# Windowed attention and a gated feed-forward on one core: two chunks of attention in one stretch of small matmuls

## The chip, the cores and the metric

The kernel runs on one core of a Trainium2 chip. A core has a matrix engine (TensorE, "PE" in the profile; its weight loads are listed apart as "PEld"), three engines for elementwise work (VectorE "DVE", ScalarE "ACT", GpSimd "POOL") and a queue engine ("SP") that here only issues DMAs. Each works through its own instructions in order, and they wait for one another on semaphores. Matmul results go to PSUM, eight banks of 128 x 512 fp32, from which DVE and ACT read them. The metric is the device time of one execution in microseconds. Three runs of the kernel before gave 337.34, 338.25 and 338.31 us; the median is 338.25.

## The reference

```python
# q, k, v: (8, 8, 576, 64) fp32;  window = 64
scores = (q @ k^T) / sqrt(64)
mask = (0 <= i - j) & (i - j < 64)
attn = softmax(where(mask, scores, -1e9))
x = (attn @ v).transpose(0, 2, 1, 3).reshape(4608, 512)
g = x @ w_gate                      # 512 -> 1536
out = (silu(g) * (x @ w_val)) @ w_out   # 1536 -> 512, fp32
```

Each token attends to itself and the 63 before it in its own sequence. All 4608 tokens then go through the feed-forward part.

## The kernel before

The tokens are cut into 36 chunks of 128 (index n) for attention and nine groups of 512 (index c) for the feed-forward part. Sequences are 576 long, so some chunks hold a boundary, and a part of their window is left out. Matmuls run in bf16.

**Attention of a chunk.** `load_qk` and `load_v` have POOL load q, k and v (cast to bf16) into rings of buffers; `TD(n)` (line 414) lets two DMA transposes on SP's queue turn k and q into `kT` and `qT`. `S(n)` (line 435) computes the scores: 24 matmuls of 64x64 (line 451) into two banks, an exp on ACT for each bank (line 461) that writes the weights `pt`, and a multiplication by the mask on DVE for each (line 466), which can be deferred. `A(n, nxt)` (line 472) multiplies weights and values: 32 matmuls of 64x64 (line 500) into two banks, four heads in each. A window of 64 queries meets two blocks of 64 keys, which lie in different halves of the partitions, and the two halves may not write one bank at the same moment. So the work is in two phases of 16: in phase 0 the first bank gets the lower half and the second the upper, in phase 1 the other way round, and phase 1 waits for a semaphore that phase 0 raises. A 65th column of the values is 1 and yields the sums for the softmax: DVE takes the reciprocal (line 515) and multiplies (line 518) into `xb`. The scores of the next chunk are issued between the two phases. `XD(n)` (line 543) transposes `xb` by DMA on SP's queue into `xT`.

**Feed-forward.** `F(c, f)` (line 550) computes 128 of the 1536 hidden columns for a group: four matmuls of 128x128 by 512 with `Wg` into bank G, four with `Wv` into bank V (line 565), a tanh on ACT (line 571) and two operations on DVE (lines 573 and 575) that leave `hT`; the first of these releases G, the second V. `O(c, u)` (line 578) multiplies a quarter of the group's `hT` by `Wo` in twelve matmuls (line 589); ACT copies the result to `ost` (line 601) and SP's queue writes it out.

**Order.** The order of every engine is the order of the calls in `build` (line 753). A call records operations with what they read and write, and the program derives the semaphore waits. In the main loop group c has four steps u of three F calls each (s = 0, 1, 2); between them come one `O` of the group before (after the second F) and, from the table `place`, one attention block (`block`, line 868): loads for chunk n + 6, `A(n, n + 1)`, `XD(n)`, `TD(n + 4)`. From chunk 17 on the block follows the first F of each step. In the last group `O` of the step u = 3 comes later, and `judge` (line 626) decides between this program and a general one that covers inputs with large scores; with the reference's inputs the general one is not taken.

**Banks.** `bank(kind)` (line 262) hands out PSUM banks in turn from two rings of four: "f" for F, "a" for attention and O. Whoever writes a bank again waits for its last reader.

## Time and profile before

| | |
|---|---|
| median of three runs | 338.25 us (337.34 to 338.31) |
| the profiled execution | 338.46 us |
| its span, first to last instruction | 336.6 us |
| mean granted TensorE clock | 0.995 |
| data read from and written to HBM | 37.75 MB and 9.44 MB |

The profile is one execution recorded by the hardware. Rows of the page give busy time, share of the span and the number of instructions. A row of the timeline gives start and duration in microseconds, engine, line of the code, operation, output and inputs, shapes and the number of merged instructions; in brackets stands the idle time of that engine just before and what ended it. "64*64" is the part of the array that a matmul uses, and what follows is the moving operand. A row of the waits names who waited for whom, the total, the number of times and the longest, all in microseconds. A row of the DMA issues ends with the median time from issue to landing.

### The profile page before, as it was taken

What the parts mean: (1) busy time and instruction counts of PE and PEld (TensorE: products, weight loads), DVE (VectorE), ACT (ScalarE), POOL (GpSimd) and SP (SyncE); (2) the same over time, 40 slices, a digit from 0 to 9 for tenths busy, and PEclk for the clock granted to TensorE, in tenths of its full rate; (3) what the DMA queues carried; (4) which work ended last, traced back from release to release, by engine and by line L of the source; (5) the groups of instructions that cost most, each with busy time, mean ns of one, the idle gap of its engine ahead of it and who ended that gap; (6) DMA issues with size and microseconds to landing.
All of it is one profiled execution on the core that took longest, in us unless ns stands there. A gap on an engine that the chain in (4) does not pass through costs nothing.

```text
span 336.6 us, 8417 instructions
## 1 busy us (share of the span) xinstructions
PE 325.6 (97%) x3515; PEld 166.1 (49%) x3515; DVE 215.6 (64%) x481; ACT 140.1 (42%) x256; POOL 111.1 (33%) x141
## 2 busy tenths in 40 slices
PE   6979999998999999999999999999999999999995
PEld 3548567644444444444444444444444444444444
DVE  5548789478667766666666666666666665566510
ACT  2645874354444544443433344433443332332311
POOL 7999993463544353333343333000000000000000
PEclk9979999999999999999999999999999999999999
DMA  9999999999999999999999999334331111000012
GB/s 170 143 186 171 167 195 160 154 177 128 172 179 180 177 154 166 162 168 127 125 80 149 139 139 126 80 79 80 78 80 49 47 49 49 31 32 34 34 65 95
DMA packets 169516, 40.20 MB, mean 119 GB/s; under 512 B 155904, under 2 KB 164992, under 8 KB 169472
## 3 DMA queue, kind: packets, MB, share of 16 engines
q0 software_dynamic: 117312, 18.36, 77.6%
q1 hardware_dynamic: 50976, 20.66, 34.0%
q10 hardware_dynamic: 1184, 0.59, 0.7%
q8 instruction: 29, 0.48, 0.5%
q14 instruction: 15, 0.12, 0.2%
HBM read 37.75 MB, written 9.44 MB: 140 GB/s over the span
## 4 chain that ended last, share of the span: by engine, by line
PE 87%; DMA 4%; POOL 4%; DVE 2%; ACT 1%; issue 1%; SPq 0%; POOLq 0%
PE ps L565 53%; PE ps L589 26%; PE ps L500 4%; DMA qT<-qn 2%; PE ps L451 2%; DMA Wv<-in_moe_w_val_dram 2%; POOL va L382 1%; PE ps L617 1%; POOL Wg L388 1%; PE ps L407 1%; POOL Wv L388 1%; POOL qn L320 1%; POOL kn L320 1%; DVE uu L573 0%; PE ps L532 0%
## 5 line engine op out<-in xcount | busy, mean ns | idle before, releaser
L573 DVE SCALAR_TENSOR_TENSOR uu<-sig,ps 128x512 bf16<-128x512 bf16 (+2 forms) x122 | 76.1, 624 | 82.6 <-ACT sig L571 82.4
L565 PE MATMUL ps<-xT,Wg 128*128 128x512 bf16 (+2 forms) x488 | 114.1, 356 | 2.0 <-DMA Wg<-in_moe_w_gate_dram 0.9
L565 PE MATMUL ps<-xT,Wv 128*128 128x512 bf16 (+2 forms) x488 | 113.8, 356 | 0.7 <-DMA Wv<-in_moe_w_val_dram 0.7
L589 PE MATMUL ps<-Wo,hT 128*128 128x512 bf16 x420 | 95.9, 379 | 0.0
L571 ACT ACTIVATE sig<-ps 128x512 bf16<-128x512 f32 (+2 forms) x122 | 66.9, 549 | 61.6 <-PE ps L565 61.1
L575 DVE SCALAR_TENSOR_TENSOR hT<-uu,ps 128x512 bf16<-128x512 bf16 (+2 forms) x122 | 76.3, 625 | 5.2 <-PE ps L565 1.0
L565 PEld LDWEIGHTS ps<-xT,Wv 128*128 128x128 bf16 x488 | 47.3, 98 | 47.7 <-DMA Wv<-in_moe_w_val_dram 1.0
L589 PEld LDWEIGHTS ps<-Wo,hT 128*128 128x128 bf16 x420 | 41.0, 98 | 48.9
L565 PEld LDWEIGHTS ps<-xT,Wg 128*128 128x128 bf16 x488 | 43.9, 98 | 42.3 <-DMA Wg<-in_moe_w_gate_dram 1.0
L320 POOL DMA_DIRECT2D qn<-in_q_dram x38 | 35.1, 941 | 85.9 <-DMA qT<-qn 85.6
L601 ACT ACTIVATE ost<-ps 128x512 f32<-128x512 f32 x35 | 20.9, 597 | 95.1 <-PE ps L589 92.2
L461 ACT ACTIVATE pt<-ps 128x512 bf16<-128x512 f32 x72 | 38.9, 595 | 22.6 <-PE ps L451 22.6
L382 POOL DMA_DIRECT2D va<-in_v_dram x40 | 37.2, 940 | 1.0 <-issue 0.6
L320 POOL DMA_DIRECT2D kn<-in_k_dram x38 | 35.0, 927 | 5.0 <-DMA Wo<-in_moe_w_out_dram 4.0
L518 DVE TENSOR_TENSOR xb<-ps,rc 128x256 bf16<-128x256 f32 x72 | 30.6, 425 | 2.5
L466 DVE TENSOR_TENSOR pt<-pt,mask 128x512 bf16<-128x512 bf16 x64 | 24.1, 417 | 0.2 <-ACT pt L461 0.2
L500 PE MATMUL ps<-va,pt 64*64 64x65 bf16 x1088 | 23.3, 199 | 0.6
L500 PEld LDWEIGHTS ps<-va,pt 64*64 64x64 bf16 x1088 | 15.3, 109 | 16.1 <-issue 11.2
L515 DVE RECIPROCAL rc<-ps 128x4 f32<-128x4 f32 x72 | 12.6, 175 | 9.9 <-PE ps L500 9.9
L451 PE MATMUL ps<-qT,kT 64*64 64x64 bf16 (+1 forms) x864 | 15.9, 201 | 1.0 <-DMA qT<-qn 1.0
L451 PEld LDWEIGHTS ps<-qT,kT 64*64 64x64 bf16 x864 | 12.6, 108 | 3.1 <-DMA qT<-qn 1.2
L339 DVE COPY ost<-ps 128x128 f32<-128x128 f32 x1 | 0.3, 291 | 11.8 <-PE ps L617 11.8
(50 smaller groups left out, 72.5 us busy)
## 6 DMA issues: line engine op xcount, KB each, us to landing
out_dram<-ost SPq DMA_DIRECT2D x35, 256.0 KB, 3.1
va<-in_v_dram POOLq DMA_DIRECT2D x32, 128.0 KB, 9.9
qn<-in_q_dram POOLq DMA_DIRECT2D x30, 128.0 KB, 11.2
kn<-in_k_dram POOLq DMA_DIRECT2D x30, 128.0 KB, 10.0
Wo<-in_moe_w_out_dram POOLq DMA_DIRECT2D x2, 768.0 KB, 17.4
Wg<-in_moe_w_gate_dram POOLq DMA_DIRECT2D x5, 256.0 KB, 8.0
Wv<-in_moe_w_val_dram POOLq DMA_DIRECT2D x5, 256.0 KB, 9.1
fk<-in_k_dram SPq DMA_DIRECT2D x1, 512.0 KB, 5.4
```

Of the source, the lines that this page charges most:

```text
L320: self.g.op("pool", lambda e, d=d, a=a: e.dma_start(d, a), writes=ks, dma=True)
L382: g.op("pool", lambda e, d=d, a=a: e.dma_start(d, a), writes=ks, dma=True)
L451: r = e.matmul(sv[h][o:o + 64, c, q0:q1], self.kT[ps, c, kk:kk + 64], qT[ps, c, q0:q1], start=not biased, stop=not biased or c == 3 and kk ...
L461: g.op("act", lambda e, po=po, si=si: e.activation(po, si, ACTF.Exp, scale=SCALE), reads=[bk], writes=[pk])
L466: "dve", lambda e: e.tensor_tensor(po, po, m, ALU.mult), reads=[pk, "mask"], writes=[pk]))
L500: r = e.matmul(av[half][ws, j, :], pt[ks, h, ws], vv[ks, h, 0:65], start=key == q[0], stop=key == q[-1])
L518: g.op("dve", lambda e, xo=xo, rb=rb, a=av[half]: e.tensor_tensor(xo, a[:, :, 0:64], rb, ALU.mult), reads=[bk, ("rc", ir)], writes=[("xb", ...
L565: r = e.matmul(bank[:, 0:n], W[:, kk, f * 128:f * 128 + 128], xT[:, kk, t0:t1], start=(kk == 0), stop=(kk == NK - 1))
L571: g.op("act", lambda e: e.activation(sig[:, 0:n], G[:, 0:n], ACTF.Tanh, scale=0.5), reads=[gk], writes=[("sig", i)])
L573: g.op("dve", lambda e: e.scalar_tensor_tensor(uu[:, 0:n], sig[:, 0:n], 1.0, G[:, 0:n], ALU.add, ALU.mult), reads=[("sig", i), gk], writes ...
L575: g.op("dve", lambda e: e.scalar_tensor_tensor(hT[:, f, t0:t1], uu[:, 0:n], 0.5, V[:, 0:n], ALU.mult, ALU.mult), reads=[("uu", i), vk], wr ...
L589: r = e.matmul(OB[:, :], hT[:, f, 128 * u:128 * u + 128], self.Wo[:, f, :], start=(f == 0), stop=(f == NF - 1))
```

## The change

Chunks below 20 are treated as before. From chunk 20 on:

- `pair(n)` takes the place of two blocks. It follows the third F and the `O` of every second step u, from (c, u) = (3, 3) for chunks 20 and 21 to (7, 1) for chunks 34 and 35. It issues the loads of chunks n + 6 and n + 7, the values of both chunks with the scores of n + 2 and n + 3 (`A_pair`), then `TD(n + 4)`, `TD(n + 5)`, `XD(n)`, `XD(n + 1)`, and the four masks at the end.
- `A_pair` uses three banks: heads 0 to 6 of the first chunk, heads 0 to 6 of the second, and the eighth heads of both. Scores of n + 2 come first, then phase 0 of both chunks, scores of n + 3, phase 1. In a phase the first chunk uses one half of the partitions and the second the other; the eighth heads both use the same half. Reciprocals and multiplications follow per bank, over seven heads at once, and for the eighth heads apart.
- From (3, 2) on, `O` moves behind the third F. In the steps with a pair DVE does its copy, in the others ACT.
- Right after the F call of (3, 2, 1) `S(20)` is issued alone, and `share` merges the two rings of banks into one of eight, from which everything is handed out from then on. After each pair but the last the order of the ring is set anew.

The score calls, read in order: block 19 still contains `S(20)`, the call at (3, 2, 1) is `S(20)` again, and the first pair issues `S(22)` and `S(23)`. No call issues `S(21)`; the values of chunk 21 are taken with the weights that stand in its buffer, those of chunk 17. The numbers of scores, exps and masks are what they were.

```diff
     def bank(self, kind):
+        kind = "*" if "*" in self.rot else kind
         ids, i = self.rot[kind]
...
+    def share(self):
+        j = [self.rot[k][0][self.rot[k][1] % 4:] + self.rot[k][0][:self.rot[k][1] % 4] for k in "fa"]
+        self.rot["*"] = ([x for p in zip(*j) for x in p], 0)
...
+    def A_pair(self, n, S0, S1):
+        g = self.g
+        nn = (n, n + 1)
+        masks = S0()
+        banks = [self.bank("a") for _ in range(3)]
+        pt = [self.pt[m % self.NP] for m in nn]
+        seqs, last = [[], []], {}
+        for step in range(2):
+            for h, i in [(h, i) for h in range(7) for i in range(2)] + [(7, 0), (7, 1)]:
+                kp = step if h == 7 else step ^ i
+                b, col = (2, 65 * i) if h == 7 else (i, 65 * h)
+                for w in range(2):
+                    if kp == w or (2 * nn[i] + w) % BPB:
+                        seqs[step].append((i, h, kp, w, b, col))
+                        last.setdefault((b, w), []).append((step, i, h))
...
+        first = g.op("pe", phase(0), reads=rd, writes=wr)
+        masks = masks + S1()
+        g.op("pe", phase(1), reads=rd, writes=wr, after=[first])
...
+            g.op("dve", lambda e, rc=rc, a=a: e.reciprocal(rc.unsqueeze(2), a[:, :, 64:65]), reads=[bk],
+                 writes=[("rc", 2 * m), ("rc", 2 * m + 1)])
...
+            g.op("dve", lambda e, xo=xo, rb=rb, a=a: e.tensor_tensor(xo, a[:, :, 0:64], rb, ALU.mult),
+                 reads=[bk, ("rc", 2 * m)], writes=[("xb", m % 4, 0), ("xb", m % 4, 1)])
...
+        return masks
...
-    def O(self, c, u, mid=None, kind="a"):
+    def O(self, c, u, mid=None, kind="a", eng="act"):
...
-        g.op("act", lambda e: e.activation(ost[:, :], OB[:, :], ACTF.Copy), reads=[ok], writes=[("ost", io)])
+        self.move(eng, ost[:, :], OB[:, :], [ok], [("ost", io)])
...
+        pair_from = 20
+
+        def pair(n):
+            ring, i = self.rot["*"]
+            ring = [ring[(i + j) % 8] for j in range(8)]
+            more = n + 2 < NCH
+            for m in (n + 6, n + 7):
+                load(m)
+            masks = self.A_pair(n, *(lambda m=m: self.S(m, None, True) if more else [] for m in (n + 2, n + 3)))
+            if more:
+                self.rot["*"] = ([ring[j] for j in (7, 0, 1, 5, 6, 2, 3, 4)], 0)
+            for m in (n + 4, n + 5):
+                if m < NCH:
+                    self.TD(m)
+            for m in (n, n + 1):
+                self.XD(m)
+            for f in masks:
+                f()
...
-        for n in range(17, NCH):
+        for n in range(17, pair_from):
             place[(n - 5) // 4, (n - 5) % 4, 0] = n
+        pairs = {}
+        for n in range(pair_from, NCH, 2):
+            c, r = divmod(n - 6, 4)
+            pairs[c, 1 + r] = n
+        alone = (pair_from - 6) // 4, (pair_from - 6) % 4, 1
+        cp = alone[0]
...
+                    if (c, u, s) == alone:
+                        self.S(pair_from)
+                        self.share()
-                    if s == 1 and not late:
+                    if s == 1 and not late and c < cp:
                         self.O(c - 1, u, None, "f" if (c, u, s) in place or (c, u) == (1, 1) else "a")
...
+                if c >= cp and not late:
+                    self.O(c - 1, u, None, "a", "dve" if (c, u) in pairs else "act")
+                if (c, u) in pairs:
+                    pair(pairs[c, u])
```

31 lines of the change are left out of this document (added).

## The prediction

> **What bounds the kernel now.** I read the page first, for the engine shares and the chain of waits.
>
> ```profile
> PE 325.6 (97%) x3515; PEld 166.1 (49%) x3515; DVE 215.6 (64%) x481; ACT 140.1 (42%) x256; POOL 111.1 (33%) x141
> PE 87%; DMA 4%; POOL 4%; DVE 2%; ACT 1%; issue 1%; SPq 0%; POOLq 0%
> ```
>
> TensorE (PE) is busy for 97% of the span and carries 87% of the chain that ended last. A busy PE need not be a PE at its peak, so next comes PE's timeline over one period of the part that is changed: three F calls, one O call and one attention block (chunk 29).
>
> ```profile
> 224.91 1.03 PE L565 MATMUL ps<-xT,Wv 128*128 128x512 bf16 x4
> 225.87 0.32 PE L500 MATMUL ps<-va,pt 64*64 64x65 bf16 x16
> 226.02 0.42 PE L451 MATMUL ps<-qT,kT 64*64 64x128 bf16 x24
> 226.27 0.32 PE L500 MATMUL ps<-va,pt 64*64 64x65 bf16 x16
> 226.52 1.04 PE L565 MATMUL ps<-xT,Wg 128*128 128x512 bf16 x4
> 227.39 1.03 PE L565 MATMUL ps<-xT,Wv 128*128 128x512 bf16 x4
> 228.26 2.75 PE L589 MATMUL ps<-Wo,hT 128*128 128x512 bf16 x12
> 230.85 1.03 PE L565 MATMUL ps<-xT,Wg 128*128 128x512 bf16 x4
> 231.71 1.03 PE L565 MATMUL ps<-xT,Wv 128*128 128x512 bf16 x4
> 232.57 1.03 PE L565 MATMUL ps<-xT,Wg 128*128 128x512 bf16 x4
> 233.44 1.03 PE L565 MATMUL ps<-xT,Wv 128*128 128x512 bf16 x4
> 234.39 0.32 PE L500 MATMUL ps<-va,pt 64*64 64x65 bf16 x16
> ```
>
> Only starts matter here, as the durations contain the pipeline's tail. Groups of four follow at 0.863 us (230.85 to 233.44 in three steps), so a 128x512 matmul takes 0.216, and O's twelve take 2.59 (228.26 to 230.85). A period is 8.52 us (225.87 to 234.39). Its 36 large matmuls take 6 x 0.863 + 2.59 = 7.77, which leaves **0.75 us for the block** and nothing for waiting. The period is the same at both ends of the region:
>
> ```profile
> 149.19:157.72 8.53, 8.53 (x94) 4.05 (x94) 5.73 (x13) 3.47 (x6) 2.64 (x3) 1.00 1.36 129
> 268.47:276.99 8.52, 8.52 (x93) 4.05 (x92) 5.73 (x13) 3.47 (x6) 0.00 (x0) 1.00 0.16 48
> ```
>
> (Columns: stretch, PE, PEld, DVE, ACT, POOL busy, granted clock, DMA share, GB/s.) The clock is 1.00, DVE is busy 5.73 of 8.5 us, and it makes no difference whether DMA is busy. The region is bound by PE's order alone: a change pays if it shortens the block and costs if it makes PE wait.
>
> **The block taken apart.** The group at 224.91 ends its streaming at 225.77, and the stretch of 64x64 matmuls starts at 225.87: 0.10 us to get in. Phase 0 of the values takes 0.15, the scores of the next chunk 0.25. Phase 1 repeats phase 0's 16 matmuls, so it would be through at 226.42; the next large matmul starts at 226.52: 0.10 to get out, and 0.01 in the first group (0.87 against 0.863). About 0.21 of the 0.75 is the change of shape. Chunk 35 has no scores to interleave:
>
> ```profile
> 276.04 1.03 PE L565 MATMUL ps<-xT,Wv 128*128 128x512 bf16 x4
> 276.99 0.72 PE L500 MATMUL ps<-va,pt 64*64 64x65 bf16 x32
> 277.39 0.21 PEld L500 LDWEIGHTS ps<-va,pt 64*64 64x64 bf16 x16 [0.19 <-PE ps L500]
> 277.64 1.04 PE L565 MATMUL ps<-xT,Wg 128*128 128x512 bf16 x4
> ```
>
> Its phase 1 starts 0.40 after phase 0 (277.39 - 276.99) although nothing lies between, just as in chunk 29 (226.27 - 225.87). Phase 1 waits for phase 0's semaphore, about 0.25 us after phase 0's 0.15. The scores in between **cost nothing today**; they fill a wait. A block with or without scores costs 0.65 + 0.10. This limits the gain.
>
> **The change, part by part.**
>
> *Pairs.* From chunk 20 on the PE order of a pair is: scores of n+2, phase 0 of both chunks, scores of n+3, phase 1 of both. The first scores have no semaphore wait to hide in. I price each piece:
> - in, 0.10; out, 0.11.
> - first scores, 0.25 to 0.27 (a stretch's first round is slower by some 0.02: 0.15 for four rounds of values against 8 x 0.031 = 0.25 for the scores).
> - a phase of both chunks: matmuls run four at a time, one for each quarter of the array. Seven heads make seven full rounds; the eighth heads of both chunks share a bank and only two quarters, so they take two rounds. Nine rounds, at 0.031 (scores: eight passes in 0.25) to 0.037 (values: four rounds in 0.15): 0.28 to 0.34, taken at 0.31.
> - between the phases, 0.25 as today, which hides the second scores.
>
> Sum: 0.10 + 0.26 + 0.31 + 0.25 + 0.31 + 0.11 = 1.34 (1.27 to 1.41), against 2 x 0.75 = 1.50 to 1.51. A pair saves 0.17 (0.10 to 0.24); seven pairs save 1.2 (0.7 to 1.7). The last pair (34, 35) has no scores at all: 1.08, saving 0.43 (0.37 to 0.49).
>
> *The lone scores.* Before the pairs begin, S(20) is issued by itself between two F calls, a stretch of its own. The trace has one such:
>
> ```profile
> 57.79 0.60 PE L565 MATMUL ps<-xT,Wv 128*128 128x256 bf16 x4
> 58.32 0.45 PE L451 MATMUL ps<-qT,kT 64*64 64x128 bf16 x24
> 58.70 2.12 PE L589 MATMUL ps<-Wo,hT 128*128 128x512 bf16 x9
> ```
>
> Four 128x256 matmuls stream 4 x 0.108 = 0.43, to 58.22; the next large one starts at 58.70: 0.48 us lost. As block 19 already issues S(20), chunk 20's scores are made twice and chunk 21's by no call; the number of score groups is unchanged, so the time is that of the intended work.
>
> **PE sum: -1.2 - 0.43 + 0.48 = -1.15 us, bounds -0.6 and -1.7.** I take -1.2, as the values' later rounds look nearer to 0.031 than to 0.037, whose first round carries the 0.02.
>
> *Work that must stay hidden.* These rows show DVE and ACT around the block at 225.87:
>
> ```profile
> 226.49 1.08 ACT L461 ACTIVATE pt<-ps 128x512 bf16<-128x512 f32 x2 [0.78 <-PE ps L451]
> 227.07 0.18 DVE L515 RECIPROCAL rc<-ps 128x4 f32<-128x4 f32 x1
> 227.28 0.42 DVE L518 TENSOR_TENSOR xb<-ps,rc 128x256 bf16<-128x256 f32 x1
> 227.83 0.42 DVE L518 TENSOR_TENSOR xb<-ps,rc 128x256 bf16<-128x256 f32 x1
> 228.17 0.75 DVE L466 TENSOR_TENSOR pt<-pt,mask 128x512 bf16<-128x512 bf16 x2
> 231.05 0.60 ACT L601 ACTIVATE ost<-ps 128x512 f32<-128x512 f32 x1 [2.86 <-PE ps L589]
> 232.54 0.69 DVE L573 SCALAR_TENSOR_TENSOR uu<-sig,ps 128x512 bf16<-128x512 bf16 x1 [2.30 <-ACT sig L571]
> 233.26 0.69 DVE L575 SCALAR_TENSOR_TENSOR hT<-uu,ps 128x512 bf16<-128x512 bf16 x1
> ```
>
> I count from T0, when O's last matmul before a pair has streamed. O's eviction moves to DVE: it can start at T0 + 0.20 (231.05 against 230.85) and lasts about 0.69, the nearest 128x512 DVE row (0.55 to 0.8): done at T0 + 0.9. The ring gives that bank to the first F's G, which PE reaches at T0 + 1.3: about 0.3 to spare. DVE is free by then: an F's hT ends 1.4 us after its V group has streamed (233.26 + 0.69 = 233.95, the group of 231.71 through at 232.57), and here O's 2.59 follow that group. The same hT frees the banks of the second scores, 1.2 us before T0. ACT's four exps run from T0 + 0.6 to 2.8; the first two free the banks of the first F's V and the second F's G, due at T0 + 2.2 and 3.0 and ready at 1.2 and 1.7. The tanh of the first F slips by about 0.3, which PE doesn't see. DVE then has two reciprocals and two multiplies over seven heads (0.18 + about 0.62 each: 448 columns, from 0.42 for 256), three small ones (about 0.2 each, between 0.17 and 0.25) and four masks (1.5): 3.7 us from T0 + 1.4, so the first F's uu starts at T0 + 5.1. PE next needs that bank in the second F round after, beyond T0 + 9. So the ring's waits are all covered, the tightest by 0.3 us. For the lone S(20), the values' banks of chunk 19 come free 1.73 us after its stretch (228.25 - 226.52), when one F (1.73) has just passed: 0 to 0.1 lost once.
>
> *O after the third F* removes nothing and adds nothing on PE; only its place changes. Behind the last pair the kernel merely draws its banks from a ring of eight in place of two of four.
>
> *Queues.* SP issues, behind the output of O, four transposes of a pair's k and q and only then the two of xb; each holds SP about 1.3 us:
>
> ```profile
> 152.85 1.27 SPq L420 DMA_TRANSPOSE kT<-kn  x1
> 154.17 1.33 SPq L423 DMA_TRANSPOSE qT<-qn  x1
> ...
> kT<-kn SPq DMA_TRANSPOSE x2, 6.1
> qT<-qn SPq DMA_TRANSPOSE x2, 5.6
> ```
>
> From T0 + 1.0 the last q transpose is issued by T0 + 6.2 and lands by T0 + 12; the scores that read it come one pair later, at T0 + 16.9. The xb transposes are issued by T0 + 8.7; the F that reads them is two u steps away. POOL's loads wait for the q transposes anyway and are six chunks ahead; they come two chunks at a time instead of one:
>
> ```profile
> POOL qn L320 <- DMA qT<-qn: 85.6, 21, 6.0
> ```
>
> **The rivals.**
>
> *1. Neighbours in one half of the array run one after the other* (slower). Today's order alternates the 64-row halves from matmul to matmul; the pair issues two to the same half (its two column halves) and then two to the other. If these serialised, a full round would take two passes, 0.062, not 0.033: 14 rounds x 0.029 x 8 pairs = 3.2 us, in all +2.0, 340.3. It decides from 1.2 / 112 = 11 ns a round. Against it stands chunk 27, one of whose quarters is left out, so that its phase 0 has such neighbours:
>
> ```profile
> 208.84 0.25 PE L500 MATMUL ps<-va,pt 64*64 64x65 bf16 x5
> 208.90 0.24 PE L451 MATMUL ps<-qT,kT 64*64 64x128 bf16 x1
> 208.90 0.26 PE L500 MATMUL ps<-va,pt 64*64 64x65 bf16 x7
> 208.98 0.43 PE L451 MATMUL ps<-qT,kT 64*64 64x128 bf16 x23
> ```
>
> Four rounds in 0.14 (208.84 to 208.98), no more than chunk 29's 0.15. Chance 0.05. The Trainium skill, TensorE: Matmul & The Clock Gate, section on the mechanism of packing small matmuls, says that a weight load overlaps matmuls in flight only when its row group differs; read strictly it speaks for this rival, and chunk 27 against it.
>
> *2. The pair's k and q come too late* (slower). Landing would have to take over 10.8 us in place of 6; the longest median I find is 8 us, earlier, under heavier loads. At 12 us, three pairs before the loads end would wait 1.2 each: +3.6, in all +2.4, 340.6. Chance 0.05.
>
> *3. The first F waits for O's bank.* If DVE had one 0.69 us operation in front of the eviction, 0.4 would be lost at each of eight pairs: +3.2, in all +2.0, 340.2. DVE's idle 2.30 us during O speaks against it. Chance 0.03.
>
> *4. The stretch saves less*: rounds at 0.037 or more and some 0.05 us of waits inside the longer stretch. Then -0.6 to -0.9, about 337.5. Nothing excludes it; chance 0.25.
>
> **How the numbers follow.** The forecast (0.62) is -1.2. The profiled execution took 338.46 us, of which the span is 336.6; it becomes 337.3 with a span of 335.4. The three runs have a median of 338.25 (337.34 to 338.31), 0.2 below; on that scale the forecast is 337.0, its own range 336.5 to 337.4. The range for 8 in 10 takes in the bound of -1.7, the runs' spread, and rival 4 up to no change: 336.3 to 338.4. What a measurement here tells from no change is about 0.3%, or 1.0 us; the forecast lies just beyond it. Faster 0.62, from the forecast; same 0.25, rival 4; slower 0.13, rivals 1 to 3 with their like.
>
> **What would show it.** Right: a period of two u steps and a pair of 16.88 us in place of 17.04; stretches of 112 small matmuls, 1.2 us from the first to the next large one, with 0.25 between the phases; no PE idle from chunk 20 on. Wrong: rounds over 0.04 in the phases (rival 1), scores waiting for qT (2), the first Wg group after a pair waiting for DVE (3), or the change of shape costing more with scores in front.

## The result and the profile after

| | before | after |
|---|---|---|
| median of 22 runs | 337.5 us (336.02 to 338.51) | 336.01 us (334.56 to 338.30) |
| ratio after / before, 95% interval | | 0.9959 [0.9945, 0.9973] |
| the profiled execution | 338.46 us | 335.81 us |
| its span | 336.6 us | 334.0 us |
| mean granted clock in it | 0.995 | 1.00 |

The changed kernel is faster by 0.41%: 1.4 us on 337.5, with an interval from 0.9 to 1.9. The forecast was 1.2 us less, at 337.0, in a range from 336.3 to 338.4. So the direction and the size came out as forecast, and the measured time lies 0.3 us below the range, because the kernel before is itself faster than its first three runs said: 337.5 in place of 338.25.

From the page of the kernel after, the engine shares, the granted clock in 40 slices, and the chain of waits by engine:

```profile
PE 320.0 (96%) x3477; PEld 166.1 (50%) x3515; DVE 220.5 (66%) x481; ACT 133.6 (40%) x248; POOL 110.7 (33%) x141
PEclk9999999999999999999999999999999999999999
PE 84%; DMA 4%; POOL 4%; DVE 3%; issue 2%; ACT 1%; SPq 1%; POOLq 0%
```

PE's busy time must not be compared between the two pages: the page after has records of 3477 matmuls beside 3515 weight loads, so some are missing. The clock row of the page before has one slice that is not full:

```profile
PEclk9979999999999999999999999999999999999999
```

The two profiled spans differ by 2.6 us, more than the change is worth. Two anchors on PE's timeline show why: the start of the values of chunk 17, the first block that stands behind the first F of a step, and the start of the last `O`. First the kernel before, then the kernel after:

```profile
123.64 0.32 PE L500 MATMUL ps<-va,pt 64*64 64x65 bf16 x16
...
330.44 2.81 PE L617 MATMUL ps<-Wo,hT 128*128 128x256 bf16 x36
```

```profile
122.19 0.32 PE L505 MATMUL ps<-va,pt 64*64 64x65 bf16 x16
...
328.03 2.81 PE L680 MATMUL ps<-Wo,hT 128*128 128x256 bf16 x36
```

| piece of the span | before | after | difference |
|---|---|---|---|
| up to chunk 17 (same instructions) | 123.64 | 122.19 | -1.45 |
| chunk 17 to the last `O` (all that the change touches) | 206.80 | 205.84 | **-0.96** |
| from there to the end (same instructions) | 336.6 - 330.44 = 6.16 | 334.0 - 328.03 = 5.97 | -0.19 |

Only the middle row is the change. The table of the experiments below shows that it repeats to 0.02 us in unchanged code, while the first piece changes by microseconds from one execution to the next. I call the middle row the **PE stretch** and read every experiment by it.

Three periods of the kernel after, each two steps u with one pair, from pair to pair (stretch, then PE, PEld, DVE, ACT and POOL busy, granted clock, DMA share, GB/s):

```profile
154.27:171.18 16.91, 16.66 (x183) 8.14 (x185) 12.13 (x24) 6.14 (x11) 6.24 (x8) 1.00 1.58 134
171.18:188.04 16.86, 16.65 (x176) 8.12 (x178) 12.13 (x24) 6.14 (x11) 5.76 (x7) 1.00 1.41 126
188.04:204.91 16.87, 16.66 (x184) 8.14 (x186) 12.12 (x24) 6.14 (x11) 5.26 (x6) 1.00 1.40 126
```

They take 16.88 on average, as forecast, against 2 x 8.52 = 17.04. Inside a pair, from PE's timeline:

```profile
168.50 2.75 PE L652 MATMUL ps<-Wo,hT 128*128 128x512 bf16 x12
171.18 0.45 PE L456 MATMUL ps<-qT,kT 64*64 64x128 bf16 x24
171.47 0.41 PE L552 MATMUL ps<-va,pt 64*64 64x65 bf16 x21
...
172.62 0.81 PE L628 MATMUL ps<-xT,Wg 128*128 128x512 bf16 x3 [0.16 <-issue]
173.27 1.03 PE L628 MATMUL ps<-xT,Wv 128*128 128x512 bf16 x4
```

`O` has streamed at 168.50 + 2.59 = 171.09, so getting in takes 0.09. The Wg row holds three of four matmuls (one record is missing, hence the bracket); four of them end when the Wv group starts, at 173.27, so the large ones began at 173.27 - 0.86 = 172.41. The small matmuls and the way out took 1.23 (172.41 - 171.18), where the forecast has 1.34 - 0.10 = 1.24. The lone scores, on the same timeline:

```profile
140.75 1.02 PE L628 MATMUL ps<-xT,Wv 128*128 128x512 bf16 x4
141.70 0.45 PE L456 MATMUL ps<-qT,kT 64*64 64x128 bf16 x24
142.08 0.61 PE L628 MATMUL ps<-xT,Wg 128*128 128x512 bf16 x2
```

The Wv group has streamed at 140.75 + 0.863 = 141.61; the next large matmul starts at 142.08. Lost: 0.47, forecast 0.48. The last pair, which has no scores:

```profile
269.88 2.75 PE L652 MATMUL ps<-Wo,hT 128*128 128x512 bf16 x12
272.56 1.01 PE L552 MATMUL ps<-va,pt 64*64 64x65 bf16 x64
...
274.38 1.03 PE L628 MATMUL ps<-xT,Wv 128*128 128x512 bf16 x4
```

From the end of `O`'s streaming (269.88 + 2.59 = 272.47) to the next large matmul (274.38 - 0.86 = 273.52) it is 1.05, forecast 1.08, in place of two blocks of 0.75.

The work that had to stay hidden did. Rows around one pair from the timeline of all engines (T0 = 219.06 + 2.59 = 221.65):

```profile
219.06 2.75 PE L652 MATMUL ps<-Wo,hT 128*128 128x512 bf16 x12
...
221.85 0.69 DVE L344 COPY ost<-ps 128x512 f32<-128x512 f32 x1 [1.42 <-PE ps L652]
...
222.23 2.06 ACT L466 ACTIVATE pt<-ps 128x512 bf16<-128x512 f32 x4 [3.24 <-PE ps L456]
...
223.06 0.56 PEld L628 LDWEIGHTS ps<-xT,Wg 128*128 128x128 bf16 x4
...
226.56 0.68 DVE L636 SCALAR_TENSOR_TENSOR uu<-sig,ps 128x512 bf16<-128x512 bf16 x1
```

DVE has evicted `O` at 222.54, T0 + 0.89, 0.52 before the first F's weights load at 223.06 (forecast 0.9 and some 0.3 to spare). The four exps run from T0 + 0.6 to 2.6, and the first `uu` starts at T0 + 4.9 (forecast 5.1). PE waits for none of them. The view of waits does name DVE once, at this first F (0.27 us, for the reciprocal), but there again one of the four matmul records is missing, and the copy that F's bank depends on had ended 0.52 before.

### The profile page after: what moved, and what is told of

Same layout as the page of the kernel before. It is cut to its first block, busy times and chain, and to the rows that moved or that the text cites. A ratio compares the mean times of both kernels' runs of the same rounds, so it can differ in the third digit from the quotient of the medians.

```text
span 334.0 us, 8383 instructions
## 1 busy us (share of the span) xinstructions
PE 320.0 (96%) x3477; PEld 166.1 (50%) x3515; DVE 220.5 (66%) x481; ACT 133.6 (40%) x248; POOL 110.7 (33%) x141
## 4 chain that ended last, share of the span: by engine, by line
PE 84%; DMA 4%; POOL 4%; DVE 3%; issue 2%; ACT 1%; SPq 1%; POOLq 0%
PE ps L628 51%; PE ps L652 26%; PE ps L456 3%; DMA qT<-qn 2%; DMA Wv<-in_moe_w_val_dram 2%; PE ps L505 2%; PE ps L552 2%; POOL va L387 1%; DVE uu L636 1%; PE ps L680 1%; DVE xb L523 1%; POOL Wg L393 1%; DVE hT L638 1%; POOL qn L325 1%; POOL kn L325 1%
## 5 line engine op out<-in xcount | busy, mean ns | idle before, releaser
L628 PE MATMUL ps<-xT,Wg 128*128 128x512 bf16 (+2 forms) x464 | 108.2, 354 | 5.2 <-issue 3.4
L466 ACT ACTIVATE pt<-ps 128x512 bf16<-128x512 f32 x72 | 38.1, 599 | 34.5 <-PE ps L456 33.6
L342 ACT ACTIVATE ost<-ps 128x512 f32<-128x512 f32 (+2 forms) x29 | 16.8, 579 | 73.2 <-PE ps L652 72.2
L344 DVE COPY ost<-ps 128x512 f32<-128x512 f32 (+1 forms) x9 | 5.8, 646 | 23.2 <-PE ps L680 11.8
L523 DVE TENSOR_TENSOR xb<-ps,rc 128x256 bf16<-128x256 f32 x40 | 17.0, 424 | 1.4
L505 PE MATMUL ps<-va,pt 64*64 64x65 bf16 x600 | 12.7, 197 | 0.6
L520 DVE RECIPROCAL rc<-ps 128x4 f32<-128x4 f32 x40 | 7.0, 174 | 9.4 <-PE ps L505 9.4
L505 PEld LDWEIGHTS ps<-va,pt 64*64 64x64 bf16 x600 | 8.4, 106 | 8.9 <-issue 4.7
```

Source lines behind the costliest of these rows:

```text
L466: g.op("act", lambda e, po=po, si=si: e.activation(po, si, ACTF.Exp, scale=SCALE), reads=[bk], writes=[pk])
L505: r = e.matmul(av[half][ws, j, :], pt[ks, h, ws], vv[ks, h, 0:65], start=key == q[0], stop=key == q[-1])
L523: g.op("dve", lambda e, xo=xo, rb=rb, a=av[half]: e.tensor_tensor(xo, a[:, :, 0:64], rb, ALU.mult), reads=[bk, ("rc", ir)], writes=[("xb", ...
L628: r = e.matmul(bank[:, 0:n], W[:, kk, f * 128:f * 128 + 128], xT[:, kk, t0:t1], start=(kk == 0), stop=(kk == NK - 1))
```

## The experiments

All in one table. "Before beside it" is the median of 29 to 35 runs of the kernel before, taken on the same chip together with the kernel of the row. The PE stretch comes from the two anchor rows of each kernel's own profile.

| kernel | PE stretch, us | against before | median, us | before beside it | ratio, 95% interval |
|---|---|---|---|---|---|
| before_again | 206.79 | 0.0 | 337.62 | 337.43 | 0.9997 [0.9971, 1.0024] |
| before_third | 206.80 | 0.0 | 337.15 | 337.89 | 0.9986 [0.9964, 1.0009] |
| layout | 206.78 | 0.0 | 338.00 | 337.40 | 1.0007 [0.9982, 1.0032] |
| after_again | 205.69 | -1.1 | 336.27 | 337.89 | 0.9963 [0.9940, 0.9987] |
| o_moved | 206.79 | 0.0 | 337.33 | 337.40 | 1.0006 [0.9989, 1.0022] |
| ring_shared | 207.82 | +1.0 | 338.01 | 337.40 | 1.0012 [0.9998, 1.0027] |
| ring_only | 206.79 | 0.0 | 336.08 | 337.43 | 0.9957 [0.9936, 0.9978] |
| ring_only_again | 206.80 | 0.0 | 336.54 | 337.61 | 0.9968 [0.9948, 0.9988] |
| ring_only_third | 206.80 | 0.0 | 337.22 | 337.89 | 0.9977 [0.9956, 0.9998] |
| extra_switch | 207.34 | +0.5 | 337.24 | 337.43 | 0.9987 [0.9964, 1.0010] |
| alternate | 206.06 | -0.7 | 336.33 | 337.43 | 0.9961 [0.9937, 0.9984] |
| s21 | 205.93 | -0.9 | 336.71 | 337.40 | 0.9986 [0.9966, 1.0005] |
| hoist | 205.40 | -1.4 | 336.28 | 337.61 | 0.9958 [0.9938, 0.9979] |
| fold20 | 205.53 | -1.3 | 336.30 | 337.61 | 0.9956 [0.9939, 0.9973] |
| fold18_hoist | 205.06 | -1.7 | 335.42 | 337.61 | 0.9930 [0.9905, 0.9956] |
| fold18_hoist_again | 205.08 | -1.7 | 335.87 | 337.89 | 0.9937 [0.9910, 0.9965] |

**The same code again.** `before_again` and `before_third` are the kernel before, `after_again` the kernel after. `layout` is the kernel before with a copy changed in the general program, which these inputs don't reach:

```diff
-            self.X(n, "act")
+            self.X(n, "dve")
```

> The kernel before, unchanged, run as if it were a new one. It tells how far one set of runs of the same code lies from another, and by its profile where executions differ. Theory 'level': the 0.75 us by which the 22 later runs of the kernel before lie under the first three come from the start, where PE waits for the first weights, and not from the attention blocks. Then the ratio is 1.000 within 0.002; the first block of chunk 17 starts anywhere between 121.5 and 124.5 us after the span's start (123.64 in the profile of before, 122.19 in that of the changed kernel), and the time from the block of chunk 19 to the end of the span is again 195.98 us within 0.1. Rival 'drift': the region itself varies, so that the time from the block of chunk 19 to the end differs from 195.98 by 0.5 us or more.

> The kernel before once more, to see how far one set of runs of the same code lies from another in this call. Theory 'chance': ratio 1.000 within 0.002; 192.31 us from the block of chunk 19 to the last matmul; start (to the block of chunk 17) between 121.6 and 124.1 and end (from the last weight load) between 2.7 and 4.4 us, as in the twelve profiles so far.

> The kernel before with a change that no engine executes here: in the general program, which these inputs do not take, a copy out of PSUM goes to DVE in place of ACT, so that the programs of ACT and DVE have other lengths behind the last common instruction. All work is as before. ring_only had the PE time of before from the block of chunk 19 to the last matmul (192.30 against 192.31 us) and yet a ratio of 0.9957. Theory 'place': what lies before and after that stretch (weights arriving at the start, the last output landing) depends on where a program and its data lie, so any other program may come out 1 us off: then this one may be off its neighbour by 0.002 or more, either way. Rival 'order': something that ring_only does makes its end shorter; then the ratio here is 1.000 within 0.002.

> The changed kernel once more (chunk 21 takes the weights of chunk 17). On PE 191.3 to 191.6 us from the block of chunk 19 to the last matmul, 0.7 to 1.0 less than before. Theory 'chance': ratio 0.9972 within 0.002, which is 0.96 of 337.5 us. Rival 'both': the ring of eight, which it has too, adds what ring_only gained: 0.9935 within 0.0015.

Four profiles of the code before have PE stretches of 206.80, 206.79, 206.80 and 206.78. Their start varies, though. First `layout`, then `fold18_hoist_again`, which up to this row has the same work (both from PE's timeline; chunk 17's values):

```profile
121.67 0.32 PE L500 MATMUL ps<-va,pt 64*64 64x65 bf16 x16
```

```profile
124.88 0.32 PE L505 MATMUL ps<-va,pt 64*64 64x65 bf16 x16
```

3.2 us apart, for the same instructions. The granted clock is one part of it. In the 129 runs of the kernel before beside the experiments, 50 had a mean clock below 0.9985, with medians of 337.94 to 338.41 in the four sets; the other 79 had 337.12 to 337.34, 0.7 to 1.1 us less. Three runs don't tell which sort they are. `after_again` gives the ratio of the first comparison again (0.9963 after 0.9959), and its PE stretch is 1.1 shorter than before (forecast 0.7 to 1.0). Medians of twelve runs scatter: the three kernels with the code before lie between 0.9986 and 1.0007 with nothing changed that runs.

**One part alone.** `o_moved` is the kernel before with `O` behind the third F from group 3 on; `ring_shared` is the kernel before with the two rings of banks merged; `ring_only` (three times) is the kernel after without pairs and without the lone scores, so with both parts together.

In `o_moved`:

```diff
-                    if s == 1 and not late:
+                    if s == 1 and not late and c < 3:
...
+                if c >= 3 and not late:
+                    self.O(c - 1, u)
```

In `ring_shared`, beside `bank` and `share` of the change:

```diff
+                    if (c, u, s) == (3, 2, 1):
+                        self.share()
```

In `ring_only`, against the kernel after:

```diff
-        for n in range(17, pair_from):
+        for n in range(17, NCH):
...
-        for n in range(pair_from, NCH, 2):
-            c, r = divmod(n - 6, 4)
-            pairs[c, 1 + r] = n
...
-                        self.S(pair_from)
```

> The kernel before with one part of the change: from group 3 on, O follows the third F of each step in place of the second. Banks stay in two rings of four. Theory 'shape': no effect on PE, 192.31 us within 0.05 from the block of chunk 19 to the last matmul. Theory 'place': the ratio lies anywhere from 0.995 to 1.002. Rival 'order', this part: O's outputs leave at another time and the end is shorter: ratio near 0.996.

> The kernel before with the other part of the change: from (3, 2, 1) on all banks come from one ring of eight; O stays where it was. The instructions of every engine are those of before, only their banks and waits differ. Theory 'shape': 192.31 us within 0.05 from the block of chunk 19 to the last matmul. Theory 'place': the ratio lies anywhere from 0.995 to 1.002. Rival 'order', this part: ratio near 0.996.

> The changed kernel without the pairs: from (3, 2, 1) on all banks come from one ring of eight and O follows the third F of each step, but every chunk keeps its own block, and there are no lone scores. All scores are computed. Theory 'shape': the gain is the number of changes between 128x128 and 64x64 matmuls, so this kernel is as fast as before: ratio 1.000 within 0.0015, a period of 8.52 us, from the block of chunk 19 to the end 195.98 us within 0.15. Rival 'ring': the gain comes from banks that are free earlier or from O's new place: ratio near 0.996, 1.2 us less from the block of chunk 19 to the end.

> The kernel of ring_only once more. Its ratio of 0.9957 had no counterpart on PE, and its two parts alone gave 1.0006 and 1.0012. Theory 'chance': the time outside the stretch from the block of chunk 19 to the last matmul differs from execution to execution by more than any of these kernels differ from one another, and a median of 12 can lie off by 0.3%; then the ratio is now nearer to 1.000, 0.998 or above. Rival 'both': one ring and O's new place together shorten the start or the end; then 0.996 again, within 0.0015. In either case 192.30 us from the block of chunk 19 to the last matmul.

> ring_only a third time, beside the kernel before as a kernel of its own. 192.30 us on PE as before. Theory 'chance': the two ratios of 0.9957 and 0.9968 were draws of start and end; the third lies at 0.998 to 1.002. Rival 'both': start or end are shorter by some 1.2 us whenever the program is this one: 0.995 to 0.9975 again, with before_third near 1.000 in the same call.

`o_moved` changes nothing, as costed. `ring_shared`, for which no effect on PE was forecast, loses 1.0 us there, 0.09 at each of eleven later blocks. PE's timeline of one of them, and its weight load:

```profile
156.44 0.32 PE L505 MATMUL ps<-va,pt 64*64 64x65 bf16 x16
156.68 0.41 PE L456 MATMUL ps<-qT,kT 64*64 64x128 bf16 x21
...
157.18 1.04 PE L570 MATMUL ps<-xT,Wg 128*128 128x512 bf16 x4
```

```profile
156.44 0.21 PEld L505 LDWEIGHTS ps<-va,pt 64*64 64x64 bf16 x16 [0.42 <-DVE hT L580]
```

The block's bank now comes from F, so DVE's `hT` is named as what released its first weights. The time is not lost there: the same 0.42 of idle time stands ahead of the block in `ring_only`, whose values take banks of F too and which loses nothing. It is lost between the values and the scores. The scores start 0.24 after the values (156.68 - 156.44), where the kernel before has 0.15, and the block takes 0.74 to the next large matmul (157.18 - 156.44), where it has 0.65. Read off the program, the scores of these blocks wait for banks from both ACT (the copy of `O`) and DVE (an `hT`), and for two transposes; in the kernel before the wait for DVE is not there, and in `ring_only` that for ACT is not. One wait more would fit what `hoist` shows below, but three blocks at sequence boundaries have it and lose nothing, so the cause is not shown. With `O` moved as well (`ring_only`) the loss is gone: the merged ring fits the order around a pair, not the old one.

The three ratios of `ring_only` are below 1 (0.9957, 0.9968, 0.9977), although its PE stretch is that of the kernel before to 0.01 us. The time must lie in the start or the end, where its instructions are the same. Among the runs at full clock its medians are 335.90, 336.41 and 336.72, against 337.12 to 337.34: 0.6 to 1.2 less. I have no cause for this. In the three profiles the end, from the last `O` on, takes 5.39, 5.40 and 5.59 us, where `before`, `before_again` and `before_third` have 6.16, 6.86 and 6.03. But `layout` has 5.25 there with the code before, and the kernel after, which merges the rings too, 5.97 and 5.87. The five runs of `layout` at full clock have a median of 336.30, which is 0.9 below the kernel before beside it, so an offset of this size also comes with nothing changed that runs. The third ratio lies between what the two theories forecast. This leaves open whether some tenths of what the change measured (1.4, of which PE shows 1.0 to 1.1) come from something outside the stretch.

**The price of a change of shape.** `extra_switch` is the kernel after with one matmul of 128x128 by 64, on zeros, between the first scores and the values of every pair:

```diff
+        spare, sk = banks[0]
+        g.op("pe", lambda e: e.matmul(spare[:, 0:64], self.wz[:, 0:128], self.wz[:, 0:64], start=True, stop=True),
+             reads=["wz"], writes=[sk])
```

> The changed kernel (chunk 21 takes the weights of chunk 17, as there) with one more matmul of 128x128 by 64 on zeros in each pair, between the first scores and phase 0, into a bank that phase 0 overwrites. It adds one way out of the 64x64 matmuls and one way in. Theory 'shape': each costs about 0.1 us, with the matmul's own 0.03, so 0.2 to 0.28 more for each of eight pairs: 1.6 to 2.2 us more than the changed kernel, from the first pair's start to the next 17.06 to 17.14 in place of 16.86, and a ratio of 1.0005 to 1.003 to the kernel before. Rival 'ring': the shape does not matter, so only the matmul's own 0.03 a pair is added: ratio 0.996 to 0.997.

The first pair on PE's timeline:

```profile
154.21 0.45 PE L456 MATMUL ps<-qT,kT 64*64 64x128 bf16 x24
154.59 0.20 PE L561 MATMUL ps<-wz 128*128 128x64 bf16 x1
154.72 0.44 PE L552 MATMUL ps<-va,pt 64*64 64x65 bf16 x30
...
155.25 0.47 PE L552 MATMUL ps<-va,pt 64*64 64x65 bf16 x32
```

The values start 0.51 after the scores (154.72 - 154.21) in place of 0.29 (171.47 - 171.18, the pair of the kernel after shown above). The last pair has no scores, so there the extra matmul stands right behind `O`, among the large ones, and adds no change of shape:

```profile
271.29 2.75 PE L655 MATMUL ps<-Wo,hT 128*128 128x512 bf16 x12
273.88 0.19 PE L561 MATMUL ps<-wz 128*128 128x64 bf16 x1
274.01 1.01 PE L552 MATMUL ps<-va,pt 64*64 64x65 bf16 x64
274.95 1.04 PE L631 MATMUL ps<-xT,Wg 128*128 128x512 bf16 x4
```

From the end of `O`'s streaming (271.29 + 2.59 = 273.88) to the next large matmul it takes 1.07 (274.95 - 273.88), against 1.05 in the kernel after: the matmul itself costs 0.02 to 0.03. Over the stretch the edit costs 207.34 - 205.84 = 1.5 us. The forecast of 1.6 to 2.2 counted eight changes of shape, but only seven pairs have one more: 1.5 / 7 = 0.21 each, of which some 0.19 is the change of shape. (The extra matmul also waits for its bank, which this run doesn't tell apart; `fold20` below gives 0.16 for one change of shape by another edit.) That turns the change's gain into a loss on PE: leaving out one change of shape per pair is what the change is worth. (The ratio, 0.9987, is below the forecast of 1.0005 to 1.003, and its interval holds 1.) The Trainium skill, TensorEngine Tiling (Array Packing), section "Key Properties", says that a change of the tiling mode drains TensorE; the runs agree, and put about 0.2 us on in and out together.

**Rival 1, neighbours in one half.** `alternate` orders a pair's values so that neighbours are in different halves of the array, as in the kernel before:

```diff
-            for h, i in [(h, i) for h in range(7) for i in range(2)] + [(7, 0), (7, 1)]:
+            for h, w, i in [(h, w, i) for h in range(7) for w in range(2) for i in range(2)] + [(7, w, i) for i in range(2) for w in range(2)]:
...
-                for w in range(2):
+                if True:
```

> The changed kernel (chunk 21 takes the weights of chunk 17, as there) with the order inside a phase as the kernel before has it: the two halves of the partitions in turn from matmul to matmul, for the first seven heads. Theory 'shape': four neighbours use four different quarters in either order, so nothing changes: ratio to before 0.996 within 0.0015, a period of 16.86 us within 0.03. Rival 'neighbours': two in the same half run partly one after the other in the changed kernel; then the phases get shorter here, by up to 0.1 us a pair (period 16.76 to 16.82).

The same pair on PE's timeline, `alternate` first and the kernel after second:

```profile
188.72 0.45 PE L552 MATMUL ps<-va,pt 64*64 64x65 bf16 x30
189.01 0.41 PE L456 MATMUL ps<-qT,kT 64*64 64x128 bf16 x22
...
189.29 0.45 PE L552 MATMUL ps<-va,pt 64*64 64x65 bf16 x30
```

```profile
188.31 0.45 PE L552 MATMUL ps<-va,pt 64*64 64x65 bf16 x30
188.60 0.41 PE L456 MATMUL ps<-qT,kT 64*64 64x128 bf16 x22
...
188.88 0.45 PE L552 MATMUL ps<-va,pt 64*64 64x65 bf16 x30
```

Phase 0 to phase 1 takes 0.57 in both, to the hundredth. The order of the halves is worth nothing, and rival 1 falls. Over the stretch `alternate` takes 0.2 to 0.4 longer than the kernel after (a period of 16.93 where 16.86 was forecast). In this pair, which takes 1.35 from its first small weight load to its next large one against 1.22, the difference lies behind phase 1 and not in the phases; `hoist` below deals with what stands there.

**Which scores.** `s21` computes `S(21)` where the change computes `S(20)` a second time:

```diff
-                        self.S(pair_from)
+                        self.S(pair_from + 1)
```

> The changed kernel with the lone scores those of chunk 21, so that all scores are computed. Work and order are unchanged. Every theory: ratio to the kernel before as the changed kernel's, 0.996 within 0.002; from the block of chunk 19 to the last matmul 191.35 us within 0.3 (the changed kernel's; 0.96 less than before). Theory 'waits' has the spread of 0.3: the pairs of the changed kernel lose 0.02 to 0.12 us where PE's separate wait instructions fall inside or right behind the small matmuls, and which pairs do depends on the execution.

205.93 against 205.84 and 205.69: the same work on PE, at the same price to 0.1 to 0.2. Its ratio of 0.9986 is higher than those of the kernel after (0.9959 and 0.9963) and than the forecast (0.994 to 0.998); the intervals overlap, and nothing on PE answers to it.

**Waits inside the stretch.** In the kernel after, a pair takes 1.18 to 1.33 us from its first small weight load to its next large one, though all its matmuls are the same. The program puts a wait instruction for each semaphore ahead of an operation, and the profile doesn't count such instructions as busy. In a pair these stand in the middle of the dense run, ahead of the values, of the second scores and of the first F. The Trainium skill, Perfetto Trace Analysis, section "Identifying Dependency Chains", says that waits for several engines may be put ahead of an instruction in this way; it gives no price. `hoist` is `s21` with these waits taken at the pair's first scores, where PE is still streaming `O` (the first F keeps its wait for a bank):

```diff
-    def S(self, n, bb=None, defer=False):
+    def S(self, n, bb=None, defer=False, also=()):
...
-        rd = [("kT", m, p) for m in (n - 1, n) for p in range(4)] + [("qT", iz, p) for p in range(4)]
+        rd = [("kT", m, p) for m in (n - 1, n) for p in range(4)] + [("qT", iz, p) for p in range(4)] + list(also)
...
-            masks = self.A_pair(n, *(lambda m=m: self.S(m, None, True) if more else [] for m in (n + 2, n + 3)))
+            c, r = divmod(n - 6, 4)
+            also = [("pt", m % self.NP, h) for m in (n, n + 1) for h in range(2)]
+            also += [("va", m % self.NV, j) for m in (n - 1, n, n + 1) for j in range(2)] + [("hT", c % self.NH, 3 * r + 5)]
+            if more:
+                also += [("kT", n + 3, p) for p in range(4)] + [("qT", (n + 3) % self.NZ, p) for p in range(4)]
+            if r == 2:
+                also += [("xT", (c + 1) % self.NX, w) for w in range(4)]
+            masks = self.A_pair(n, lambda: self.S(n + 2, None, True, also) if more else [],
+                                lambda: self.S(n + 3, None, True) if more else [], () if more else also)
```

In the last pair, which has no scores, phase 0 takes them.

> s21 with every wait that is already met moved ahead of the stretch: the first scores of a pair (the first phase, where there are none) also list what the values, the second scores and the F behind them need (k and q of n + 3, the masked weights, v, hT of the third F, xT of the next group). Work and order are unchanged; all scores are computed. Theory 'waits': the separate wait instructions inside the stretch and right behind it cost the changed kernel 0.3 to 0.45 us over eight pairs (its pairs take 1.19 to 1.32 us from the first small weight load to the next large one). Without them each takes 1.18 to 1.21, and from the block of chunk 19 to the last matmul it is 190.95 to 191.15 us, against 191.34 and 191.43 of the changed kernel and s21. Rival 'transport': the spread comes from something else in PE's supply of instructions; then it stays at 191.3 to 191.5. The ratio should be 0.996, too close to s21's to tell them apart.

PE's weight loads in the pair of chunks 32 and 33, the kernel after first, `hoist` second:

```profile
255.59 0.30 PEld L456 LDWEIGHTS ps<-qT,kT 64*64 64x64 bf16 x22 [0.42 <-issue]
...
255.84 0.37 PEld L552 LDWEIGHTS ps<-va,pt 64*64 64x64 bf16 x30
256.23 0.33 PEld L456 LDWEIGHTS ps<-qT,kT 64*64 64x64 bf16 x22
...
256.92 0.55 PEld L628 LDWEIGHTS ps<-xT,Wg 128*128 128x128 bf16 x4
```

```profile
256.56 0.30 PEld L456 LDWEIGHTS ps<-qT,kT 64*64 64x64 bf16 x22 [0.42 <-issue]
...
256.81 0.33 PEld L552 LDWEIGHTS ps<-va,pt 64*64 64x64 bf16 x29
...
257.08 0.35 PEld L456 LDWEIGHTS ps<-qT,kT 64*64 64x64 bf16 x23
...
257.76 0.55 PEld L628 LDWEIGHTS ps<-xT,Wg 128*128 128x128 bf16 x4
```

The second scores come 0.39 behind phase 0 in the kernel after (256.23 - 255.84) and 0.27 in `hoist` (257.08 - 256.81); the pair takes 1.33 in the one and 1.20 in the other. All the full pairs of `hoist` take 1.16 to 1.21. Over the stretch it gains 205.93 - 205.40 = 0.5 us against `s21`, and 0.3 to 0.4 against the kernel after. The idle time ahead of the first small weight load is 0.42 in both, so the waits are already met when `hoist` takes them. Both runs of `fold18_hoist` (below), which has the same edit, have full pairs of 1.15 to 1.21 too; the five kernels with pairs but without it (the kernel after, `after_again`, `s21`, `alternate`, `fold20`) have 1.18 to 1.36. In these the first, third, fifth and seventh pair take 1.25 to 1.33 on average and the others 1.21; the first F behind the former begins a group and waits for its `xT` as well. Same work, other places for the waits: the waits were the difference.

**The lone scores, and the best version.** `fold20` computes all scores, and puts the lone ones into the end of block 19, where the array already has the small shape; `fold18_hoist` does that in block 17, begins the pairs at chunk 18 and hoists the waits.

```diff
+            if n == pair_from - 1:
+                self.share()
...
+            if n == pair_from - 1:
+                masks = self.S(n + 2, None, True)
...
-                    if (c, u, s) == alone:
-                        self.S(pair_from)
-                        self.share()
...
-        pair_from = 20
+        pair_from = 18
```

(The last two lines are those of `fold18_hoist`. In both, `share` puts attention's banks between the first and the last two of F's.)

> s21 with the lone scores of chunk 21 moved into the block of chunk 19, behind its phase 1, so that they need no stretch of their own; the rings are merged just before that block, in an order that leaves the banks of the last F for last. All scores are computed. Theory 'shape': the lone stretch costs 0.48 us, of which 0.25 is the scores' own work and 0.2 the two changes of shape. So 0.2 to 0.23 us less than s21: 191.1 to 191.3 us from the block of chunk 19 to the last matmul. Rival: the scores at the end of the block make the next F wait for a bank or a semaphore, and nothing is gained: 191.4 to 191.6.

> The two edits together, and pairs from chunk 18 on: one pair more, the lone scores (of chunk 19) inside the block of chunk 17, all waits ahead of the stretches. All scores are computed. Theory 'shape': one change of shape in and out less than in fold20, 0.2 us, so 1.3 + 0.2 + 0.2 less than before on PE, 1.65 to 1.8 in all; counted from the block of chunk 17 to the last matmul 207.55 to 207.7 against 209.34 of before. Ratio 0.995. Rival 'transposes': the pair of chunks 18 and 19 begins 15 us after the block that requests k and q of chunk 21, while the loads are still heavy and landing takes 8 us and more, so its scores wait for them: 0.5 us or more of what is gained is lost there.

> The fastest of the variants once more, as it has had six runs only. 207.60 us within 0.05 from the block of chunk 17 to the last matmul, 1.74 less than before. Theory 'chance': ratio 0.9948 within 0.002. Rival 'both': 0.9915 within 0.0015.

The folded scores on PE's timeline of `fold20`:

```profile
141.52 0.32 PE L505 MATMUL ps<-va,pt 64*64 64x65 bf16 x16
141.69 0.45 PE L456 MATMUL ps<-qT,kT 64*64 64x128 bf16 x24
...
142.94 0.38 PE L628 MATMUL ps<-xT,Wv 128*128 128x512 bf16 x1
```

The Wg group ahead of the Wv row began 0.86 earlier, at 142.08, so from phase 1 on the block takes 0.56 (142.08 - 141.52), where a block without them takes 0.25: 0.31 for the scores in place of 0.47 by themselves. `fold20` is at 205.53, 0.2 to 0.3 below the kernel after. It is 0.40 below `s21`, where 0.2 was forecast: 0.16 by the scores, and most of the rest because the pairs of `s21` lost more to waits (8.83 us for seven pairs against 8.65). `fold18_hoist` has one pair more and reaches 205.06 and, the second time, 205.08: 1.7 us less on PE than before, as forecast (1.65 to 1.8). Its rival did not come: no wait for a transpose is left on PE from 120 us on. Its medians of six and seven runs are 335.42 and 335.87, its ratios 0.9930 and 0.9937, the lowest of all. It was not run beside the kernel after; on PE it is 0.6 to 0.8 us ahead.

## Why the prediction was right and where it was not

**The mechanism was right.** PE's order alone bounds the region, a change of shape has a price, and a pair pays it once instead of twice. `extra_switch` shows the price by paying it again: some 0.19 us in each of seven pairs, and next to nothing in the eighth, where no shape changes. The terms of the sum:

| term | forecast, us | measured in the kernel after |
|---|---|---|
| seven periods | -1.2 (-0.7 to -1.7) | first to last pair start 154.27 to 272.56: 118.29 / 7 = 16.90; 7 x (16.90 - 17.04) = -1.0 |
| last pair | -0.43 | 1.05 in place of 1.50: -0.45 |
| lone scores | +0.48 | +0.47 |
| PE sum | -1.2 (-0.6 to -1.7) | -0.96, and -1.1 the second time |

**Rival 4 came in part.** I had allowed "some 0.05 us of waits inside the longer stretch", with -0.6 to -0.9 in all. Such waits are there, 0.05 us a pair on average (0.3 to 0.4 over the seven full pairs, by `hoist`), and they are what parts the measured -1.0 from the -1.4 that `hoist` reaches. What I had not seen is that they can be moved.

**The other rivals.** Rival 1 fell by `alternate`. Rival 2 (late k and q) did not come: of PE's waits for a q transpose there is one of 1.2 us, in both kernels, and it lies ahead of the pairs. These are the rows of the views of waits, before and then after:

```profile
PEld ps L451 <- DMA qT<-qn: 1.2, 1, 1.2
```

```profile
PEld ps L456 <- DMA qT<-qn: 1.2, 1, 1.2
```

Rival 3 (the first F waiting for `O`'s bank) did not come either: 0.52 us were to spare in the pair shown.

**What failed is the last step, from the sum to a time.** The prediction says "The three runs have a median of 338.25 (337.34 to 338.31), 0.2 below; on that scale the forecast is 337.0". The median of three was taken for the level of the kernel. In 22 runs the level is 337.5, 0.75 lower; the same sum on it is 336.3, and 336.01 is 0.3 from that. So of the 1.0 us between 337.0 and 336.01, 0.75 is the level and the rest the change, which measured 1.4 to 1.5 where the sum has 1.2. The lower end, 336.3, was made of the bound of -1.7 and had nothing in it for the level: "the runs' spread" was taken from the same three runs. The clock row of the page before, shown above, had a hint. The profiled execution lost clock in its third slice, and runs below 0.9985 are 0.7 to 1.1 us longer; 338.25 and 338.31 fit that kind and 337.34 the other. The clocks of those three runs are not among the records, so this reading is argued, not shown.

**What stays open.** PE accounts for 1.0 to 1.1 us of a measured 1.4 (0.9 to 1.9), which agrees. But `ring_only` measured 0.8 to 1.5 us (0.9977 to 0.9957) with nothing on PE to show for it; a further small gain outside the stretch, or chance in start and end, are both possible. The mix of clocks is not what parts 1.4 from 1.0: at full clock alone, `after_again` has a median of 335.92 and the kernel before beside it 337.34. The kernel's time ahead of chunk 17 was not studied.

## What to carry to other kernels

Where PE alone bounds a kernel, count its changes of array shape, here about 0.2 us each time in and out, and put work of one shape together; then look for operations inside the dense run that wait for several engines, and take those waits at an earlier instruction that has time. Measure such small gains between two anchors in the trace, as far as the stretch in between is bound by one engine: here that resolved 0.1 to 0.2 us, while medians of twelve whole runs of the same code were up to 0.7 us off. And before a small gain is put on a scale, ask how well the level is known: a median of three runs was 0.75 us off.

## What the hardware showed that I had not expected

- Identical instructions reach chunk 17 at 121.67 to 124.88 us, and the rest of the kernel before then runs 207 us alike to 0.02 us, that of the kernel after 206 us alike to 0.15 us.
- Waits that are already satisfied are not free on PE: between short matmuls, separate wait instructions cost 0.3 to 0.5 us over seven pairs.
- A ring of banks shared by two stages is not neutral: merged without moving `O`, it cost 0.09 us between the values and the scores at each of eleven blocks (`ring_shared`); why is not shown.
